# Weight halves through the PSUM bank, third halves in other steps, loads in mid-step: a fused attention and two-MLP kernel

## The chip, the cores and the metric

One core of a Trainium2 chip runs the whole program. The metric is device time in microseconds from the first to the last instruction and what lies around it, as the median of several runs. TensorE (PE) does the matmuls and transposes, VectorE (DVE) and ScalarE (ACT) read and write both memories, GpSimd (POOL) works on SBUF alone, SyncE (SP) issues nearly all DMAs.

## What is computed

Decayed linear attention in blocks, then two MLPs in a row, all in float32 (the kernel splits each float32 matmul operand in a high and a low part and adds three products):

```python
x = _attn_ref(q, k, v, lam)          # B=2, H=8, S=768, D=64; state decays by lam per position
x = x.transpose(0, 2, 1, 3).reshape(1536, 512)
h = x @ w_in;  g = h * clip(h + 3, 0, 6) / 6;  x = g @ w_out          # 1536x512 -> 2048 -> 512
h = x @ w2_in; P = a0 + a1*h + a2*h**2 + a3*h**3
Q = 1 + |b0|*|h| + |b1|*h**2; out = (P / (Q + 1e-6)) @ w2_out
```

The weights arrive as 64-bit floats. The kernel loads the two 32-bit words of each and builds a float32 from them on ScalarE and VectorE.

## The kernel before

Attention runs over 12 chunks of 128 tokens (CH = 128, NCH = 12, six chunks for each batch entry). The first MLP runs in blocks of 512 tokens (TB), so the first block can start when four chunks (CPT) are done. The work has three stretches. A prologue does chunks 0 to 4 and the first projections. Then a loop `for s in range(1, att_steps)` (s = 1 to 7) overlaps one attention chunk c = 4 + s with one projection mm1(s + 1), one output product mm2(s - 1) and the weight conversion for later steps. Behind it a stage of mm1 and mm2 alone runs through the rest of both MLPs. The document counts steps by s.

Everything stands under `tc.manual_schedule()`: each engine runs its instructions in the order in which the code issues them, and waits are set from the tiles that they read and write. So the order of calls in a step is the order in each engine's queue.

**TensorE in a step**: mm1(s + 1) (12 matmuls, L232, into the bank hb[(s + 1) % 2]), att_t (eight transposes of q and k into the banks X and Y, L368 and L373), the first half of mm2(s - 1) (L248), att_s (scores into X and Y, L405), att_q (query times carried state, L425, into both hb banks; not for chunk 6), att_kv (key times value, L434, into the upper half of hb[(s + 1) % 2]; not for chunks 5 and 11), att_v (masked scores times v, L443, into both hb banks), the second half of mm2. In the loop `ba` is hb[(s + 1) % 2] and `bb` is hb[s % 2].

**The others**: act1 is relu on ScalarE (L281) and a product on VectorE (L284); att_t runs between them and has two ScalarE copies, qT (L369) and kT (L374). att_m is two products with the decay mask on VectorE (L412). att_qd (L391) multiplies qT by the decay table on GpSimd; its result qd is read by att_q. att_kd (L381) does the same for k. att_x copies the chunk's output out of the two hb banks (ScalarE L466, VectorE L468). att_state updates the carried state from the bank (VectorE L452 or L454) and decays it on GpSimd (L457). act_fin splits the activation in high (ScalarE L293) and low (GpSimd L294).

**Weight jobs**: job j (j of 2 or more) holds one slice of w_in, part (j, 0), for mm1(j), and one of w_out, part (j, 1), for mm2(j - 2). load_job puts both DMAs on SyncE's queue, into the raw buffers raw0 and raw1, two of each. A part goes through four calls:

- conv_c: the upper words, scaled by ScalarE (L167), clamped by VectorE (L169), into the tile ta (w_in) or tb (w_out), two buffers each.
- the low bits: conv_l has ScalarE write them into a PSUM bank (L179) and VectorE shift and merge from there (L182); the raw buffer is then free. conv_s has ScalarE write them over the raw words (L194) and VectorE merge from SBUF (L196); the sign is read from the raw buffer later.
- conv_w: VectorE merges the sign (L206).
- conv_h: ScalarE casts to the high part (L219), GpSimd subtracts for the low part (L220).

A step takes two parts, pa and pb, from a list, and in the steps named in MORE a third one, pc, at its end. `held` keeps parts whose conv_h comes in the next step. Jobs are loaded at the end of a step, one job ahead of the next part that is due.

In the page's names the tiles of the splits and halves appear as wih and wil (high and low of w_in), woh and wol, gh and gl.

Of the kernel before, what the change touches and what calls it, by code (L numbers as in the profile page):

```python
# [10 lines left out]
U32 = mybir.dt.uint32  # L11
BF16 = mybir.dt.bfloat16
AF = mybir.ActivationFunctionType
ALU = mybir.AluOpType
# [5 lines left out]
LAG2 = 3  # L20
WARM = (8, 3, 2, 4)
EARLY_LOW = 3
MORE = (5, 6)
SIGN = 0x80000000


# [6 lines left out]
def fused_kernel(  # L33
# [14 lines left out]
    nc = tc.nc  # L48
# [4 lines left out]
    KD = DM // 128  # L53
# [99 lines left out]
    def conv_c(j, i, late=False, part=None):  # L153

        if i >= len(jobs[j]):
            return
        if part == "clamp":
            x = conv[j, i]
            nc.vector.tensor_scalar(out=x, in0=x, scalar1=CMAX, scalar2=-CMAX, op0=ALU.min, op1=ALU.max)
            return  # L160
        m = jobs[j][i][0]
        if late:
            x = rp.tile([128, KD, 128, 2], U32, name="raw0").bitcast(F32)
            x = x.rearrange("p k f t -> p (k f t)")[:, 0 : KD * 128].rearrange("p (k f) -> p k f", k=KD)
        else:
            x = tp.tile([128, KD, 128], F32, name="ta" if m % 2 == 0 else "tb")
        nc.scalar.activation(x, raw[j][i].bitcast(F32)[:, :, :, 1], AF.Copy, scale=EXPO)  # L167
        if part is None:
            nc.vector.tensor_scalar(out=x, in0=x, scalar1=CMAX, scalar2=-CMAX, op0=ALU.min, op1=ALU.max)  # L169
        conv[j, i] = x  # L170

    def conv_l(j, i, bank=None, part=None):
# [11 lines left out]
        )  # L184
        conv[j, i] = x, y, x.bitcast(U32)

    def conv_s(j, i, half=None):

        if i >= len(jobs[j]):
            return  # L190
        x = conv[j, i][0] if half else conv[j, i]
        y, r = x.bitcast(U32), raw[j][i]
        if not half:
            nc.scalar.activation(r[:, :, :, 0], r[:, :, :, 0], AF.Copy, scale=LOWS, bias=LOWB)  # L194
        k = slice(0, KD) if half is None else slice(KD // 2 * half, KD // 2 * half + KD // 2)
        nc.vector.scalar_tensor_tensor(  # L196
            out=y[:, k], in0=y[:, k], scalar=3, in1=r[:, k, :, 0], op0=ALU.logical_shift_left, op1=ALU.bitwise_or
        )
        conv[j, i] = x, y, r[:, :, :, 1]

    def conv_w(j, i):

        if i >= len(jobs[j]):
            return
        x, y, sg = conv[j, i]
        nc.vector.scalar_tensor_tensor(  # L206
            out=x.bitcast(U32), in0=sg, scalar=SIGN, in1=y, op0=ALU.bitwise_and, op1=ALU.bitwise_or
        )

    def conv_h(j, i):  # L210

        if i >= len(jobs[j]):
            return
        m, f = jobs[j][i]
        hi, lo = W["out" if m % 2 else "in", f]
        x = conv.pop((j, i))[0]
        if m % 2:
            x = x.rearrange("p a b -> p (a b)")
        nc.scalar.copy(hi, x)  # L219
        nc.gpsimd.tensor_tensor(lo, x, hi.bitcast(F32), op=ALU.subtract)  # L220
# [68 lines left out]
    def act_fin(s):  # L289
        if s in fin:  # L290
            g = fin.pop(s)
            gh, gl = g_tiles(s)
            nc.scalar.copy(gh, g)  # L293
            nc.gpsimd.tensor_tensor(gl, g, gh.bitcast(F32), op=ALU.subtract)  # L294
# [27 lines left out]
    with ExitStack() as actx:  # L322
# [15 lines left out]
        def load_nat(c, which):  # L338
            b, s0 = c // CPB, (c % CPB) * CH
            for nm in which:  # L340
                if c < CPT:
                    x = pp.tile([128, H, D], F32, name=f"{nm}n{c}")
                else:
                    x = ap.tile([128, H, D], F32, name=nm + "n", bufs=2)
                src = {"q": q, "k": k, "v": v}[nm]
                src = src[b, :, s0 : s0 + CH, :]
                if nm == "v":
                    nc.sync.dma_start(x, src.rearrange("h s d -> s h d"))
                else:

                    for e in range(2):
                        nc.sync.dma_start(x[:, 4 * e : 4 * e + 4], src[e::2].rearrange("h s d -> s h d"))
                nat.setdefault(c, {})[nm] = x
# [23 lines left out]
        def att_kd(c):  # L377
            kd = None
            if c % CPB != CPB - 1:
                kd = ap.tile([128, H, D], F32, name="kd", bufs=2)  # L380
                nc.gpsimd.tensor_tensor(  # L381
                    kd, nat[c]["k"], ktab.unsqueeze(2).to_broadcast([128, H, D]), op=ALU.mult
                )
            kds[c] = kd
# [63 lines left out]
        def att_state(c):  # L448
            if c % CPB == CPB - 1:
                return  # L450
            if c % CPB:
                nc.vector.tensor_tensor(state, decayed["S"], kvs[c], op=ALU.add)  # L452
            else:
                nc.vector.tensor_copy(state, kvs[c])  # L454
            if c % CPB != CPB - 2:
                sd = ap.tile([128, NP, D], F32, name="sd")
                nc.gpsimd.tensor_tensor(sd, state, qtab[:, :, CH - 1 : CH].to_broadcast([128, NP, D]), op=ALU.mult)  # L457
                decayed["S"] = sd

        def att_x(c, out):  # L460
            del live[c]
            o = CH * (c % CPT)
            hi, lo = (x[c // CPT][:, :, o : o + CH].rearrange("p (g h) i -> p h g i", h=2) for x in (xh, xl))
            xs = [x[:, 0 : 2 * CH].rearrange("p (g i) -> p g i", g=2) for x in out]
            for h in range(2):
                nc.scalar.copy(hi[:, h], xs[h])  # L466
            for h in range(2):
                nc.vector.tensor_tensor(lo[:, h], xs[h], hi[:, h].bitcast(F32), op=ALU.subtract)  # L468

        with tc.manual_schedule():  # L470
# [99 lines left out]
                conv_w(2, 0)  # L570

            act1(0, between)
            att_x(CPT, (X, Y))
            att_state(CPT)
            conv_c(2, 1)
            conv_h(2, 0)
            conv_l(2, 1, acc[2])
            conv_w(2, 1)
            act_fin(0)
            load_nat(6, "v")  # L580
            load_job(4)
            mm1(1)
# [4 lines left out]

            att_steps = NCH - CPT
            parts = [(j, i) for j in range(3, att_steps + 3) for i in range(2)]
            loaded, held = 4, []  # L590
            for s in range(1, att_steps):
                c = CPT + s
                ba, bb = hb[(s + 1) % 2], hb[s % 2]
                n = 3 if s in MORE else 2
                (pa, pb, *pc), parts = parts[:n], parts[n:]
                conv_c(*pa)
                if s == 1:
                    conv_l(*pa, acc[3], "low")
                    conv_h(2, 1)
                    conv_l(*pa, acc[3], "shift")  # L600
                else:
                    conv_l(*pa, bb)
                    conv_w(*pa)
                    for p in held:
                        conv_h(*p)
                    held = []
                    conv_c(*pb)
                    conv_s(*pb)
                att_kd(c)
                mm1(s + 1)  # L610
                act1(s + 1, lambda: att_t(c, (X, Y)))
                if s == 1:
                    conv_w(*pa)
                    conv_c(*pb)
                else:
                    conv_w(*pb)
                att_qd(c)
                if c + 2 < NCH:
                    load_nat(c + 2, "qk")
                mm2(s - 1, (0, 1))  # L620
                conv_h(*pa)
                if s == 1:
                    act_fin(1)
                else:
                    conv_h(*pb)
                act_fin(s + 1)
                att_s(c, (X, Y))
                for h in range(2):
                    att_m(c, (X, Y), h)
                att_q(c, (bb, ba), True)  # L630
                att_kv(c, ba[:, D * NP :])
                att_v(c, (bb, ba), False)
                if c + 2 < NCH:
                    load_nat(c + 2, "v")
                mm2(s - 1, (2, 3))
                att_x(c, (bb, ba))
                att_state(c)
                if s == 1:
                    conv_s(*pb)
                    conv_w(*pb)  # L640
                    held = [pb]
                for p in pc:
                    conv_c(*p)
                    conv_l(*p, ba)
                    conv_w(*p)
                    held.append(p)
                done = parts[0][0] if parts else att_steps + 3
                while loaded < min(done + 1, att_steps + 3):
                    loaded += 1
                    load_job(loaded)  # L650
            nc.sync.dma_start(a_sb, a_dram.unsqueeze(0).to_broadcast([128, 4]))
            nc.sync.dma_start(b_sb, b_dram.unsqueeze(0).to_broadcast([128, 2]))
            nc.scalar.activation(b1a, b_sb[:, 1:2], AF.Abs)
# [105 lines left out]
```

## Time and profile before

| | us |
|---|---|
| median of 3 runs | 593.75 (593.49 to 594.12) |
| the profiled execution | 591.63 |
| its span | 589.9 |
| TensorE matmuls busy | 578.7 |
| VectorE, ScalarE, GpSimd busy | 433.1, 386.4, 362.2 |

The granted TensorE clock is 1.00 over the whole span. TensorE is busy nearly all the time as an average, but its ends are modelled, so a busy row does not say by itself that no time is lost: the pitch from one step's first matmul to the next step's does. In a timeline row the first number is the start in us, the second the length, then engine, line, operation, output and inputs, and the count of merged instructions; in square brackets stands the idle time of that engine just before it and what ended it.

### The profile page before, as it was taken

What the parts mean: (1) busy time and instruction counts of PE and PEld (TensorE: products, weight loads), DVE (VectorE), ACT (ScalarE), POOL (GpSimd) and SP (SyncE); (2) the same over time, 40 slices, a digit from 0 to 9 for tenths busy, and PEclk for the clock granted to TensorE, in tenths of its full rate; (3) what the DMA queues carried; (4) which work ended last, traced back from release to release, by engine and by line L of the source; (5) the groups of instructions that cost most, each with busy time, mean ns of one, the idle gap of its engine ahead of it and who ended that gap; (6) DMA issues with size and microseconds to landing.
All of it is one profiled execution on the core that took longest, in us unless ns stands there. A gap on an engine that the chain in (4) does not pass through costs nothing.

```text
span 589.9 us, 8862 instructions
## 1 busy us (share of the span) xinstructions
PE 578.7 (98%) x3313; PEld 474.1 (80%) x3313; DVE 433.1 (73%) x478; ACT 386.4 (66%) x650; POOL 362.2 (61%) x290
## 2 busy tenths in 40 slices
PE   8999998999999999999999999999999999999996
PEld 6777786788888888888888888888888888888885
DVE  6688778587310111688888999999998988899990
ACT  3586667676422222678787888888876677877761
POOL 2775866566312222367666778788767767777771
PEclk9999999999999999999999999999999999999999
DMA  9997675353000000465664001000100000100001
GB/s 187 255 256 215 164 220 174 109 174 111 0 1 0 1 0 1 142 201 167 205 177 145 1 1 36 1 1 1 72 1 0 1 1 2 72 0 1 1 1 72
DMA packets 61676, 46.73 MB, mean 79 GB/s; under 512 B 39488, under 2 KB 56128, under 8 KB 61632
## 3 DMA queue, kind: packets, MB, share of 16 engines
q1 hardware_dynamic: 61344, 46.02, 27.7%
q8 instruction: 26, 0.43, 0.3%
q14 instruction: 18, 0.15, 0.1%
q10 hardware_dynamic: 288, 0.14, 0.1%
HBM read 43.00 MB, written 3.15 MB: 78 GB/s over the span
## 4 chain that ended last, share of the span: by engine, by line
PE 87%; DVE 1%; ACT 1%; DMA 1%; issue 1%; DVEq 0%; ACTq 0%
PE acc L248 43%; PE hb L232 42%; PE hb L443 1%; DMA raw<-in_moe_w_in_dram 1%; PE X L405 1%; PE hb L434 0%; DVE tb L206 0%; PE hb L425 0%; DVE at L412 0%; PE X L368 0%; PE Y L373 0%; DVE td L284 0%; ACT tc L281 0%; ACT raw L194 0%; DVE tb L196 0%
## 5 line engine op out<-in xcount | busy, mean ns | idle before, releaser
L317 DVE RECIPROCAL Y<-tb 128x512 f32<-128x512 f32 x48 | 161.3, 3361 | 1.6
L294 POOL TENSOR_TENSOR gl<-td,gh 128x512 fp32r<-128x512 f32 x84 | 108.7, 1295 | 82.8 <-ACT gh L293 82.8
L232 PE MATMUL hb<-xh,wih 128*128 128x512 f32 x384 | 102.9, 390 | 0.2 <-ACT wih L219 0.2
L232 PE MATMUL hb<-xl,wih 128*128 128x512 f32 x384 | 102.7, 389 | 0.0
L232 PE MATMUL hb<-xh,wil 128*128 128x512 f32 x384 | 102.6, 389 | 0.0
L308 POOL TENSOR_TENSOR tc<-ta,tc 128x512 f32<-128x512 f32 x48 | 62.2, 1297 | 55.4 <-ACT tc L305 55.4
L284 DVE SCALAR_TENSOR_TENSOR td<-tc,hb 128x512 f32<-128x512 f32 x48 | 32.8, 684 | 85.0 <-ACT tc L281 85.0
L232 PEld LDWEIGHTS hb<-xh,wih 128*128 128x128 f32 x384 | 71.9, 188 | 15.5 <-ACT wih L219 0.5
L232 PEld LDWEIGHTS hb<-xl,wih 128*128 128x128 f32 x384 | 72.1, 188 | 15.0
L232 PEld LDWEIGHTS hb<-xh,wil 128*128 128x128 f32 x384 | 72.1, 188 | 15.0
L281 ACT ACTIVATE tc<-hb,c 128x512 f32<-128x512 f32 x48 | 32.9, 685 | 69.3 <-PE hb L232 69.1
L248 PE MATMUL acc<-gh,woh 128*128 128x512 f32 x192 | 76.1, 396 | 0.0
L248 PE MATMUL acc<-gh,wol 128*128 128x512 f32 x192 | 74.9, 390 | 0.5 <-POOL wol L220 0.5
L248 PE MATMUL acc<-gl,woh 128*128 128x512 f32 x192 | 74.8, 390 | 0.0
L293 ACT CAST gh<-td 128x512 fp32r<-128x512 f32 x84 | 51.7, 616 | 25.1 <-DVE td L284 13.5
L309 POOL TENSOR_TENSOR td<-td,tc 128x512 f32<-128x512 f32 x48 | 64.3, 1339 | 3.8
L220 POOL TENSOR_TENSOR wil<-ta,wih 128x512 fp32r<-128x512 f32 x32 | 43.1, 1348 | 26.8 <-ACT wih L219 25.9
L302 ACT ACTIVATE X<-hb,b_sb 128x512 f32<-128x512 f32 x48 | 31.8, 662 | 39.3 <-PE hb L232 36.6
L248 PE MATMUL acc<-woh,gh 128*128 128x512 f32 x144 | 56.0, 389 | 0.0
L248 PE MATMUL acc<-wol,gh 128*128 128x512 f32 x144 | 56.0, 389 | 0.0
L248 PE MATMUL acc<-woh,gl 128*128 128x512 f32 x144 | 56.0, 389 | 0.0
L220 POOL TENSOR_TENSOR wol<-tb,woh 128x512 fp32r<-128x512 f32 x29 | 38.0, 1309 | 22.8 <-ACT woh L219 22.8
(141 smaller groups left out, 1005.8 us busy)
## 6 DMA issues: line engine op xcount, KB each, us to landing
raw<-in_moe_w_in_dram SPq DMA_DIRECT2D x32, 512.0 KB, 4.0
raw<-in_moe_w_out_dram SPq DMA_DIRECT2D x32, 512.0 KB, 4.6
qn<-in_q_dram SPq DMA_DIRECT2D x24, 128.0 KB, 3.7
kn<-in_k_dram SPq DMA_DIRECT2D x24, 128.0 KB, 3.8
vn<-in_v_dram SPq DMA_DIRECT2D x12, 256.0 KB, 4.4
out_dram<-raw SPq DMA_DIRECT2D x11, 256.0 KB, 2.0
out_dram<-raw ACTq DMA_DIRECT2D x1, 128.0 KB, 1.8
out_dram<-raw SPq DMA_DIRECT2D x1, 128.0 KB, 2.5
```

Source lines behind the costliest of these rows:

```text
L220: nc.gpsimd.tensor_tensor(lo, x, hi.bitcast(F32), op=ALU.subtract)
L232: nc.tensor.matmul(h, lhsT=w[:, kk, :], rhs=x[:, kk, :], start=i == 0 and kk == 0, stop=i == 2 and kk == KD - 1)
L248: nc.tensor.matmul(acc[d], lhsT=l, rhs=r, start=st and i == 0, stop=sp and i == 2)
L281: nc.scalar.activation(t, h, AF.Relu, bias=c3)
L284: nc.vector.scalar_tensor_tensor(out=g, in0=t, scalar=6.0, in1=h, op0=ALU.min, op1=ALU.mult)
L293: nc.scalar.copy(gh, g)
L294: nc.gpsimd.tensor_tensor(gl, g, gh.bitcast(F32), op=ALU.subtract)
L302: nc.scalar.activation(X, h, AF.Abs, scale=b_sb[:, 0:1])
L308: nc.gpsimd.tensor_tensor(b1, h2, b1, op=ALU.mult)
L309: nc.gpsimd.tensor_tensor(a1, a1, b1, op=ALU.add)
L317: nc.vector.reciprocal(Y, q1)
L405: nc.tensor.matmul(bk[h2][t, 128 * p : 128 * p + 128], lhsT=kT[r, p, t], rhs=qT[r, p, :], start=True, stop=True)
```

## The change

Second parts pb no longer use conv_s ahead of the relu. A new function conv_m has ScalarE write their low bits into the bank bb behind att_t, and VectorE merge from there; the sign (conv_w, now called by `done`) follows behind att_x, and conv_h in the next step. MORE is (4, 6) instead of (5, 6), and third parts use conv_s at the end of their step. conv_h of held parts is split: the first goes ahead of conv_c(pb), the rest between the two calls of conv_m. att_kd for a chunk moves to the end of the step before. load is called after act1 and at the end of a step; `left` holds the parts whose sign merge is not yet issued, and jobs are loaded up to one past the first of them. In step 1 conv_c(pb) moves ahead of mm1, and act_fin(1) ahead of att_qd. In the prologue att_x and att_state of chunk 4 move behind the conversion of part (2, 1). Behind the loop the remaining held parts get their conv_h.

```diff
-MORE = (5, 6)
+MORE = (4, 6)
+    def conv_m(j, i, bank, part):
+        if i >= len(jobs[j]):
+            return
+        x, r = conv[j, i], raw[j][i]
+        low = bank.bitcast(U32).rearrange("p (a b) -> p a b", a=KD)
+        if part == "low":
+            nc.scalar.activation(low, r[:, :, :, 0], AF.Copy, scale=LOWS, bias=LOWB)
+            return
+        y = x.bitcast(U32)
+        nc.vector.scalar_tensor_tensor(
+            out=y, in0=y, scalar=3, in1=low, op0=ALU.logical_shift_left, op1=ALU.bitwise_or
+        )
+        conv[j, i] = x, y, r[:, :, :, 1]
@@ prologue
             act1(0, between)
-            att_x(CPT, (X, Y))
-            att_state(CPT)
             conv_c(2, 1)
             conv_h(2, 0)
             conv_l(2, 1, acc[2])
             conv_w(2, 1)
+            att_x(CPT, (X, Y))
             act_fin(0)
+            att_state(CPT)
@@ ahead of the loop
-            loaded, held = 4, []
+            held = []
+            att_kd(CPT + 1)
+            left, loaded = list(parts), [4]
+            def load():
+                while loaded[-1] < min((left[0][0] if left else att_steps + 3) + 1, att_steps + 3):
+                    loaded.append(loaded[-1] + 1)
+                    load_job(loaded[-1])
+            def done(p):
+                conv_w(*p)
+                left.remove(p)
@@ the loop
                 else:
                     conv_l(*pa, bb)
-                    conv_w(*pa)
-                    for p in held:
-                        conv_h(*p)
-                    held = []
-                    conv_c(*pb)
-                    conv_s(*pb)
-                att_kd(c)
+                    done(pa)
+                for p in held[:1]:
+                    conv_h(*p)
+                conv_c(*pb)
                 mm1(s + 1)
                 act1(s + 1, lambda: att_t(c, (X, Y)))
                 if s == 1:
-                    conv_w(*pa)
-                    conv_c(*pb)
-                else:
-                    conv_w(*pb)
+                    done(pa)
+                    act_fin(1)
+                load()
+                conv_m(*pb, bb, "low")
+                for p in held[1:]:
+                    conv_h(*p)
+                conv_m(*pb, bb, "shift")
                 att_qd(c)
...
                 conv_h(*pa)
-                if s == 1:
-                    act_fin(1)
-                else:
-                    conv_h(*pb)
                 act_fin(s + 1)
...
                 att_x(c, (bb, ba))
+                done(pb)
+                held = [pb, *pc]
+                if c + 1 < NCH:
+                    att_kd(c + 1)
                 att_state(c)
-                if s == 1:
-                    conv_s(*pb)
-                    conv_w(*pb)
-                    held = [pb]
+                if not pc:
+                    load()
                 for p in pc:
                     conv_c(*p)
-                    conv_l(*p, ba)
-                    conv_w(*p)
-                    held.append(p)
-                done = parts[0][0] if parts else att_steps + 3
-                while loaded < min(done + 1, att_steps + 3):
-                    loaded += 1
-                    load_job(loaded)
+                    conv_s(*p)
+                    done(p)
+                    load()
+            for p in held:
+                conv_h(*p)
```

## Rows read from the trace of the kernel before

**Rows 1.** TensorE's timeline: first projection matmuls of steps 2 to 7 and behind.
```profile
44.44 1.07 PE L232 MATMUL hb<-xh,wih 128*128 128x512 f32 x4
...
54.82 1.07 PE L232 MATMUL hb<-xh,wih 128*128 128x512 f32 x4
...
64.53 1.07 PE L232 MATMUL hb<-xh,wih 128*128 128x512 f32 x4
...
74.25 1.07 PE L232 MATMUL hb<-xh,wih 128*128 128x512 f32 x4
...
83.97 1.07 PE L232 MATMUL hb<-xh,wih 128*128 128x512 f32 x4
...
95.72 1.07 PE L232 MATMUL hb<-xh,wih 128*128 128x512 f32 x4
...
106.54 1.07 PE L232 MATMUL hb<-xh,wih 128*128 128x512 f32 x4
```

**Rows 2.** TensorE's timeline: waits in steps 1, 2, 6, 7; L425 of step 4.
```profile
41.76 1.25 PE L443 MATMUL hb<-at,vn 128*64 128x128 f32 x16 [0.34 <-DVE at L412]
...
52.14 1.26 PE L443 MATMUL hb<-at,vn 128*64 128x128 f32 x16 [0.92 <-DVE at L412]
...
70.54 0.62 PE L425 MATMUL hb<-qd,state 64*64 64x128 f32 x16
...
91.02 0.33 PE L405 MATMUL X<-qT,kT 64*64 64x128 f32 x2 [1.90 <-ACT kT L374]
...
101.78 0.33 PE L405 MATMUL X<-qT,kT 64*64 64x128 f32 x2 [0.91 <-ACT kT L374]
...
103.86 1.26 PE L443 MATMUL hb<-at,vn 128*64 128x128 f32 x16 [0.48 <-DVE at L412]
```

**Rows 3.** ScalarE's timeline in step 4.
```profile
64.35 0.64 ACT L179 ACTIVATE hb<-raw 128x512 uint32<-128x512 uint32 x1 [0.24 <-DVE state L452]
...
67.52 0.69 ACT L281 ACTIVATE tc<-hb,c 128x512 f32<-128x512 f32 x1 [1.37 <-PE hb L232]
...
69.05 0.64 ACT L219 CAST wih<-ta 128x512 fp32r<-128x512 f32 x1
```

**Rows 4.** VectorE's timeline in step 4.
```profile
65.76 0.69 DVE L206 SCALAR_TENSOR_TENSOR ta<-ta,hb 128x512 uint32<-128x512 uint32 x1
66.36 0.42 DVE L169 TENSOR_SCALAR tb<-tb 128x512 f32<-128x512 f32 x1
...
68.84 1.75 DVE L206 SCALAR_TENSOR_TENSOR tb<-raw,tb 128x512 uint32<-128x512 uint32 x1
70.83 0.69 DVE L412 TENSOR_TENSOR at<-X,dmat 128x512 f32<-128x512 f32 x1 [0.23 <-PE Y L405]
```

**Rows 5.** GpSimd's timeline: qd of step 1, then step 4.
```profile
38.41 1.29 POOL L391 TENSOR_TENSOR qd<-qT,qtab 128x512 f32<-128x512 f32 x1
...
68.76 1.28 POOL L391 TENSOR_TENSOR qd<-qT,qtab 128x512 f32<-128x512 f32 x1 [2.48 <-ACT qT L369]
70.00 1.74 POOL L220 TENSOR_TENSOR wil<-ta,wih 128x512 fp32r<-128x512 f32 x1
...
72.92 1.30 POOL L294 TENSOR_TENSOR gl<-td,gh 128x512 fp32r<-128x512 f32 x1
```

**Rows 6.** ScalarE's timeline: copy of kT in step 1, then step 6.
```profile
38.12 0.60 ACT L374 COPY kT<-Y 128x512 f32<-128x512 f32 x1
...
88.21 0.67 ACT L167 ACTIVATE ta<-raw 128x512 f32<-128x512 f32 x1 [1.12 <-DMA raw<-in_moe_w_in_dram]
...
89.33 0.68 ACT L281 ACTIVATE tc<-hb,c 128x512 f32<-128x512 f32 x1
```

**Rows 7.** SyncE's timeline: the first load of job 8, end of step 4.
```profile
73.33 0.53 SPq L142 DMA_DIRECT2D raw<-in_moe_w_in_dram  x1
```

**Rows 8.** DMA issues between 73.3 and 73.8 us: count, KB, us to landing.
```profile
raw<-in_moe_w_in_dram SPq DMA_DIRECT2D x1, 512.0 KB, 4.7
```

**Rows 9.** Busy by engine, granted clock, DMA share, GB/s, behind the last matmul.
```profile
588.00:589.00 1.00, 0.00 (x0) 0.00 (x0) 0.00 (x0) 0.00 (x0) 0.00 (x0) 1.00 0.02 7
```

More of the change, by code (lines that the diff above doesn't have):

```diff
@@ L191, in conv_s @@
         x = conv[j, i][0] if half else conv[j, i]
-        y, r = x.bitcast(U32), raw[j][i]
+        r = raw[j][i]
         if not half:
             nc.scalar.activation(r[:, :, :, 0], r[:, :, :, 0], AF.Copy, scale=LOWS, bias=LOWB)
+        y = x.bitcast(U32)
         k = slice(0, KD) if half is None else slice(KD // 2 * half, KD // 2 * half + KD // 2)
```

## The prediction

> **What bounds the kernel now.** I read the timeline of TensorE first, for the first projection matmul of each step of the overlapped loop and of the stage behind it [rows 1]. Behind 106.54 us the chain of waits holds only TensorE matmuls, back to back, up to the output stores, and the change issues nothing there except one late weight split; so I count only the loop. Its steps 3, 4 and 5 start at 54.82, 64.53, 74.25 and end at 83.97: 9.7 us each, with no idle on TensorE. That is the floor of a full step. Step 2 took 10.38, step 6 11.75, step 7 10.82 us. Step 2 has no inter-chunk product (L425) and step 7 no key-value product (L434), so their floors are lower still.
>
> Second, the same timeline's waits [rows 2]: step 1 waits for VectorE's mask product at 41.76, step 2 at 52.14, step 6 for ScalarE's copy of kT at 91.02 (1.90 us), step 7 at 101.78. So TensorE bounds the kernel, and what can be won is the stalls of steps 1, 2, 6 and 7: nearly 4 us above 9.7 in the last three, and more against their lower floors. Third, the queues of the other engines in step 4, where everything fits [rows 3 to 5], then in the steps that stall [rows 6]. I count u, time since the step's first projection matmul; step 4 starts at 64.53.
>
> **The floor of a step, for placing the new work.** ScalarE's relu starts at u = 2.99, the operation behind the copies of qT and kT at 4.52 [rows 3]. TensorE's L425, first writer of the banks hb and reader of qd, starts at 6.01, and 3.71 us later the next step begins [rows 1, 2]. The first mask product starts at 6.30 [rows 4]. GpSimd's qd product runs from 4.23 to 5.51, right behind the copy of qT [rows 5]. So qd has 0.5 us to spare; whatever goes ahead of it on GpSimd shows on TensorE.
>
> **Second halves through the bank (conv_m).** Removed: the in-place ScalarE pass of conv_s ahead of the relu, and VectorE's sign merge L206 between the relu product and the mask products. That merge took 1.75 us in step 4 against 0.69 us for the one at 65.76, which reads a bank [rows 4]; it ended 0.55 us behind GpSimd's qd, which ran from 68.76 to 70.04, and the GpSimd operation behind it took 1.74 instead of 1.3 [rows 5]: operands that are all in SBUF make the two engines wait for each other, those with a bank don't. Added: a ScalarE pass into hb behind the copy of kT (u = 4.52 to 5.16, 0.64 us by the pass at 64.35 [rows 3]) and a shift on VectorE (0.69, 5.2 to 5.9). New wait: L425 writes this bank, so it waits for that shift. 5.9 against 6.01 is a tie: 0 to 0.05 us in each of steps 3, 4 and 6. I take 0.05 for all three together.
>
> The merge itself moves behind the output copies (att_x), ahead of the state update. There it meets GpSimd's split or kd product and ends 0.6 us after it at worst, near u = 0.4 of the next step. Queued behind it: the state update, and behind that ScalarE's low pass of the next first half, which wants the same bank. ScalarE then has three operations of 0.56 each (89.33 less 88.21, halved [rows 6]) before the relu, ending at about 2.4; relu at 2.99: hidden, with 0.5 us left. The second half's hi cast and lo subtraction move into the next step; they end near 3.3, and mm2 wants the low part at about 3.8. Hidden.
>
> Step 2 gains: the wait at 52.14 (u = 7.70; step 2 starts at 44.44 [rows 1, 2]) came from the mask product queued behind the slow merge. Without it that product ends at 6.30 + 0.69, so L443 starts at 7.04: −0.63 us (bounds −0.4 and −0.8).
>
> **Step 1: act_fin(1) moves ahead of att_qd.** This puts the split of g (ScalarE cast, then GpSimd L294) in front of qd on GpSimd's queue. ScalarE also gets conv_c of the second half ahead of the relu, 0.5 us more before kT: its copy starts at 38.6 instead of 38.12 [rows 6]. Cast 39.1 to 39.7, split 1.30 to 41.0, qd 1.28 to 42.3, where it started at 38.41 before [rows 5]. L425 then starts at 42.3, and L443 some 0.55 later (an estimate: L425's busy 0.62 less the overlap of its end), 42.87 instead of 41.76 [rows 2]: +1.1 us (0.9 to 1.2).
>
> **MORE = (4, 6) and the loads.** The third half now comes at the end of steps 4 and 6, by conv_s, with no wait for the bank. Step 6 needs weight job 9; its load goes out in mid-step 5, as soon as the raw buffers are free, not at the end of it. That removes the stall of step 6, whose ScalarE copy at 88.21 had waited for this transfer [rows 6]: step 6 falls from 11.75 to 9.78, −1.97 us.
>
> But step 5 now needs the first half of job 8 as its second part, and job 8 is still loaded at the end of step 4: left[0] is (7, 1) only after the third half is done. On SyncE the load stands behind the load of v, goes out at 73.33 as before [rows 7] and lands 4.7 us later [rows 8], at u = 3.8 of step 5. conv_c of that part stands ahead of the relu on ScalarE, so the relu goes from 2.99 to 4.4 and the copy of kT ends at 6.0.
>
> **Third halves' splits ahead of qd.** held[1:], set in steps 4 and 6, is split in steps 5 and 7 between the two parts of conv_m. Its GpSimd subtraction is issued ahead of att_qd and waits for a ScalarE cast that itself stands behind kT's copy and the low pass. GpSimd runs in order, so qd, which could start behind qT's copy, waits for all of that.
> Step 5: kT's copy issued at 5.44, low pass 5.92, cast 6.49 to 7.1, subtraction to 8.4, qd to 9.7; L425 at 9.73 instead of 6.01: +3.7 us. If the load landed early, the pass would still wait for the bank, freed at about 5.5 by the first half's merge: +3.3. Bounds 3.3 and 3.75.
> Step 7: relu on time. The low pass starts at 4.52 if the bank is free, at 5.15 if VectorE is late: behind the second half's merge it has the state update, two clamps (0.42), two shifts and two merges (0.69 to 0.73) [rows 4], 4.0 us in all, and one GpSimd subtraction of 1.3 that may get in between, 0.05 + 4.0 to 5.3. L425 follows at 8.35 to 8.95. Then 0.55 and, from L443 on, 2.68 (106.54 less 103.86 [rows 1, 2]): 11.58 to 12.18 instead of 10.82, +0.76 to +1.36. Middle: +1.06.
>
> The other moves cost nothing: att_kd of the next chunk goes to the end of a step, into GpSimd time that the second half's subtraction has left (cover gone: at most its own 1.3 us before the state product); att_x and att_state of the prologue run later, with the banks X and Y free about 0.9 us before the transposes that write them. The q and k loads that now stand behind mid-step weight loads on SyncE are needed a step later. The last split behind the loop has several us until mm2 reads it.
>
> **Sum**: +1.11 − 0.63 + 0.05 + 3.72 − 1.97 + 1.06 = +3.3 us on the profiled execution's 591.63 (span 589.9), which lies 2.1 us under the median of the runs. On the median of 593.75: **597.0 us**. With the bounds: +2.2 to +4.1, 595.9 to 597.8.
>
> **Rivals.**
> Faster: qd is not late. It decides at the start of qd: if GpSimd is free by u = 4.7 in steps 5 and 7 (and by 39.5 us in step 1), the queue costs nothing. Then step 1 is unchanged, step 5 loses 1.35 to the load and the bank, step 7 falls to about 9.9: −0.63 + 1.35 − 1.97 − 0.9 = −2.15, 591.6 us. For it: GpSimd is idle for over 2 us ahead of qd in an ordinary step. Against: the operation ahead is fed by ScalarE after kT's copy, and the trace has GpSimd strictly in program order. 0.13.
> Near no change: the waits in steps 5 and 7 are right, but half of them is swallowed by something that I placed too late: 0 to +1.2 us, 594.4. 0.09.
> The tie lost: ScalarE 0.3 us late in each of the three ordinary steps, L425 waits for the bank each time: +0.9 more, 597.9. 0.07.
> The change doesn't do what it says: job 9's raw buffer is freed so late (its sign is now read from it at the end) that the load is no earlier; step 6 keeps its 1.97: 599.0. Step 5 itself is then 13.4 us long, which speaks against it. 0.04.
> The clock: the granted clock is still 1.00 between 588 and 589 us, well behind the last matmul [rows 9]; the new gaps are 2.6 us or less. The Trainium skill, "TensorE: Matmul & The Clock Gate", Part 1, says that an idle TensorE is put back to half rate. By that rule the gaps of steps 5 and 7 would let the clock fall from 2.4 to 1.2 GHz. What it would do here by the rows: the 3.7 us from L425 to the end of the step would take twice as long, twice, +7.4 us, 604. 0.02.
>
> **How the numbers follow.** Forecast 0.65, rivals 0.13, 0.09, 0.07, 0.04, 0.02. A measurement of this kernel can tell about 0.2%, 1.2 us, from no change. Slower: 0.65 + 0.07 + 0.04 + 0.02 and nothing of the near case, 0.78; within: 0.09; faster 0.13. The range leaves out the faster rival and the lower half of the near one below, and the clock above: 594.4 to 599.0.
>
> **What would show it.** Right: step 5 about 13.4 us long, its L425 waiting for GpSimd's qd, qd directly behind an L220 subtraction; step 7 the same at 12; step 6 back at 9.7 with no DMA wait on ScalarE; L206 of second halves behind L468; qd of step 1 behind L294. Wrong: qd ahead of these subtractions, or L425 in step 5 before u = 8, or ordinary steps over 9.8.

## The result, and the profile after

The changed kernel took 597.41 us (median of 4 runs, 596.97 to 598.28) against 593.62 for the kernel before beside it (593.23 to 594.12): a ratio of 1.0065, 95% interval 1.0048 to 1.0083. Slower, by 3.8 us. Its profiled execution took 597.40, with a span of 595.7 us. One of the 12 runs of fill_gap, below, took 837.41 us at a mean granted clock of 0.655 and is left aside; no trace of it is kept, and its cause is open.

Its lines have moved: mm1 is L248, mm2 L264, att_s L421, att_q L441, att_kv L450, att_v L459; relu L297, copies of qT and kT L385 and L390, low pass of conv_m L194 and its shift L197, sign merge L222, casts and subtractions of conv_h L235 and L236, split of g L309 and L310, qd L407. In the other kernels the numbers differ by a few lines; the tiles tell which operation it is.

TensorE's timeline, first projection matmuls of steps 2 to 7 and behind, as in [rows 1]:

```profile
45.68 1.07 PE L248 MATMUL hb<-xh,wih 128*128 128x512 f32 x4
...
55.33 1.07 PE L248 MATMUL hb<-xh,wih 128*128 128x512 f32 x4
...
64.97 1.09 PE L248 MATMUL hb<-xh,wih 128*128 128x512 f32 x4
...
74.62 1.07 PE L248 MATMUL hb<-xh,wih 128*128 128x512 f32 x4
...
89.67 1.07 PE L248 MATMUL hb<-xh,wih 128*128 128x512 f32 x4
...
99.30 1.07 PE L248 MATMUL hb<-xh,wih 128*128 128x512 f32 x4
...
113.02 1.10 PE L248 MATMUL hb<-xh,wih 128*128 128x512 f32 x4
```

The differences between them are the step lengths. All kernels of this study, in us from the first projection matmul of a step to that of the next, each from its profiled execution (u is the time since that first matmul, as in the prediction). The ratio is to the runs of the kernel before that were made beside each: 593.62 us for the changed kernel, 593.04 for qd_first to before_fill, 592.83 for before_fin1 to thirds_late.

| kernel | 1 | 2 | 3 | 4 | 5 | 6 | 7 | median of runs, us | ratio to before |
|---|---|---|---|---|---|---|---|---|---|
| before | 10.39 | 10.38 | 9.71 | 9.72 | 9.72 | 11.75 | 10.82 | 593.62 | 1 |
| after | 11.36 | 9.65 | 9.64 | 9.65 | 15.05 | 9.63 | 13.72 | 597.41 | 1.0065 |
| qd_first | 10.28 | 9.65 | 9.65 | 9.65 | 10.85 | 9.65 | 10.34 | 589.07 | 0.9937 |
| load8_early | 11.36 | 9.64 | 9.65 | 9.65 | 14.49 | 9.62 | 13.72 | 596.66 | 1.0059 |
| fill_gap | 11.35 | 9.65 | 9.65 | 9.64 | 13.23 | 9.65 | 12.16 | 594.00 | 1.0017 |
| before_fill | 10.31 | 10.39 | 9.71 | 9.71 | 9.72 | 12.98 | 10.80 | 592.42 | 0.9991 |
| before_fin1 | 11.44 | 10.40 | 9.70 | 9.70 | 9.70 | 11.99 | 10.82 | 594.34 | 1.0025 |
| late9 | 10.31 | 9.62 | 9.63 | 9.65 | 11.12 | 12.01 | 10.34 | 591.57 | 0.9983 |
| qd_first_load8 | 10.28 | 9.65 | 9.64 | 9.65 | 10.81 | 9.67 | 10.32 | 588.65 | 0.9933 |
| thirds_late | 10.29 | 9.64 | 9.63 | 9.64 | 9.74 | 9.64 | 9.63 | 586.94 | 0.9904 |

The change won 0.73 us in step 2, 0.07 in each of steps 3 and 4 and 2.12 in step 6, and paid 0.97 in step 1, 5.33 in step 5 and 2.90 in step 7. TensorE's timeline, the waits that answer to [rows 2]:

```profile
42.57 0.67 PE L441 MATMUL hb<-qd,state 64*64 64x128 f32 x16 [1.42 <-POOL qd L407]
...
52.65 1.26 PE L459 MATMUL hb<-at,vn 128*64 128x128 f32 x16 [0.16 <-DVE at L428]
...
80.86 0.33 PE L421 MATMUL X<-qT,kT 64*64 64x128 f32 x2 [1.08 <-ACT kT L390]
...
84.51 0.67 PE L441 MATMUL hb<-qd,state 64*64 64x128 f32 x16 [2.55 <-POOL qd L407]
...
108.34 0.67 PE L441 MATMUL hb<-qd,state 64*64 64x128 f32 x16 [2.85 <-POOL qd L407]
```

In steps 1, 5 and 7 L441 waits for GpSimd's qd; in the kernel before it waited for it nowhere in the loop. GpSimd's timeline in the same three steps says why:

```profile
40.01 1.28 POOL L310 TENSOR_TENSOR gl<-td,gh 128x512 fp32r<-128x512 f32 x1 [1.38 <-ACT gh L309]
41.25 1.26 POOL L407 TENSOR_TENSOR qd<-qT,qtab 128x512 f32<-128x512 f32 x1
...
81.96 1.27 POOL L236 TENSOR_TENSOR wil<-ta,wih 128x512 fp32r<-128x512 f32 x1 [4.22 <-ACT wih L235]
83.19 1.26 POOL L407 TENSOR_TENSOR qd<-qT,qtab 128x512 f32<-128x512 f32 x1
...
105.79 1.27 POOL L236 TENSOR_TENSOR wol<-tb,woh 128x512 fp32r<-128x512 f32 x1 [3.12 <-ACT woh L235]
107.02 1.27 POOL L407 TENSOR_TENSOR qd<-qT,qtab 128x512 f32<-128x512 f32 x1
```

Each time GpSimd sat idle (1.38, 4.22, 3.12 us) in front of a subtraction that waited for a ScalarE cast, and qd stood behind it. ScalarE's timeline in step 5, then the low pass of step 7:

```profile
78.60 0.67 ACT L167 ACTIVATE ta<-raw 128x512 f32<-128x512 f32 x1 [2.22 <-DMA raw<-in_moe_w_in_dram]
79.17 0.68 ACT L297 ACTIVATE tc<-hb,c 128x512 f32<-128x512 f32 x1
...
80.69 0.67 ACT L194 ACTIVATE hb<-raw 128x512 uint32<-128x512 uint32 x1
81.26 0.63 ACT L235 CAST wih<-ta 128x512 fp32r<-128x512 f32 x1
...
104.51 0.66 ACT L194 ACTIVATE hb<-raw 128x512 uint32<-128x512 uint32 x1 [0.63 <-DVE ta L222]
```

Read downwards, the first four lines are the chain of step 5: the load of job 8 lands and is converted from u = 3.98, then relu, the copies (not shown), low pass, cast; the cast releases the subtraction at 81.96.

One thing stands in this profile that the rows of before did not have. Busy time by second of TensorE alone, with the granted clock (length, TensorE busy and count, clock, DMA share, GB/s):

```profile
84.00:85.00 1.00, 0.49 (x16) 1.00 1.30 210
85.00:86.00 1.00, 1.00 (x28) 0.73 0.27 44
86.00:87.00 1.00, 1.00 (x12) 0.50 0.06 16
87.00:88.00 1.00, 1.00 (x9) 0.50 0.00 0
88.00:89.00 1.00, 1.00 (x4) 0.57 0.07 17
89.00:90.00 1.00, 1.00 (x6) 1.00 1.02 233
```

Behind the gap of step 5 the clock fell from 2.4 GHz to half, 1.2 GHz, until shortly before 89 us. It did not fall in the gap: L441 had started at 84.51, and the clock was still whole until about 85.5. Behind the gap of step 7, where L441 started at 108.34, it did so again, until shortly before 113 us:

```profile
107.00:108.00 1.00, 0.00 (x0) 1.00 0.01 0
108.00:109.00 1.00, 0.66 (x18) 1.00 0.00 0
109.00:110.00 1.00, 1.00 (x16) 0.67 0.00 0
110.00:111.00 1.00, 1.00 (x7) 0.50 0.00 0
...
112.00:113.00 1.00, 1.00 (x4) 0.62 0.00 0
```

### The profile page after: what moved, and what is told of

Same layout as the page of the kernel before. It is cut to its first block, busy times and chain, and to the rows that moved or that the text cites. A ratio compares the mean times of both kernels' runs of the same rounds, so it can differ in the third digit from the quotient of the medians.

```text
span 595.7 us, 8871 instructions
## 1 busy us (share of the span) xinstructions
PE 581.6 (98%) x3313; PEld 476.8 (80%) x3313; DVE 429.9 (72%) x478; ACT 384.9 (65%) x650; POOL 359.7 (60%) x290
## 3 DMA queue, kind: packets, MB, share of 16 engines
HBM read 43.00 MB, written 3.15 MB: 77 GB/s over the span
## 4 chain that ended last, share of the span: by engine, by line
PE 83%; issue 2%; POOL 1%; DVE 1%; ACT 1%; POOLq 0%; ACTq 0%
PE acc L264 42%; PE hb L248 40%; PE hb L459 1%; POOL qd L407 0%; PE hb L441 0%; DVE ta L222 0%; PE hb L450 0%; POOL wil L236 0%; DVE ta L212 0%; PE X L421 0%; ACT tb L167 0%; ACT hb L179 0%; ACT raw L209 0%; ACT wih L235 0%; PE X L384 0%
## 5 line engine op out<-in xcount | busy, mean ns | idle before, releaser
L310 POOL TENSOR_TENSOR gl<-td,gh 128x512 fp32r<-128x512 f32 x84 | 108.5, 1292 | 83.7 <-ACT gh L309 83.7
L248 PE MATMUL hb<-xh,wih 128*128 128x512 f32 x384 | 102.9, 390 | 0.2 <-ACT wih L235 0.2
L248 PE MATMUL hb<-xl,wih 128*128 128x512 f32 x384 | 102.7, 389 | 0.0
L248 PE MATMUL hb<-xh,wil 128*128 128x512 f32 x384 | 102.6, 389 | 0.0
L248 PEld LDWEIGHTS hb<-xh,wih 128*128 128x128 f32 x384 | 72.0, 188 | 15.6 <-ACT wih L235 0.5
L248 PEld LDWEIGHTS hb<-xl,wih 128*128 128x128 f32 x384 | 72.1, 188 | 15.0
L248 PEld LDWEIGHTS hb<-xh,wil 128*128 128x128 f32 x384 | 72.1, 188 | 15.0
L297 ACT ACTIVATE tc<-hb,c 128x512 f32<-128x512 f32 x48 | 32.8, 683 | 68.5 <-PE hb L248 68.5
L264 PE MATMUL acc<-gh,woh 128*128 128x512 f32 x192 | 77.0, 401 | 0.0
L264 PE MATMUL acc<-gh,wol 128*128 128x512 f32 x192 | 75.6, 394 | 0.4 <-POOL wol L236 0.4
L264 PE MATMUL acc<-gl,woh 128*128 128x512 f32 x192 | 75.2, 392 | 0.0
L309 ACT CAST gh<-td 128x512 fp32r<-128x512 f32 x84 | 52.0, 619 | 25.1 <-DVE td L300 13.5
L236 POOL TENSOR_TENSOR wil<-ta,wih 128x512 fp32r<-128x512 f32 x32 | 41.6, 1301 | 35.4 <-ACT wih L235 35.4
L264 PE MATMUL acc<-woh,gh 128*128 128x512 f32 x144 | 56.0, 389 | 0.0
L264 PE MATMUL acc<-woh,gl 128*128 128x512 f32 x144 | 56.0, 389 | 0.0
L264 PE MATMUL acc<-wol,gh 128*128 128x512 f32 x144 | 56.0, 389 | 0.0
L236 POOL TENSOR_TENSOR wol<-tb,woh 128x512 fp32r<-128x512 f32 x29 | 37.5, 1293 | 23.7 <-ACT woh L235 22.7
```

The lines of the kernel that those rows point to most:

```text
L248: nc.tensor.matmul(h, lhsT=w[:, kk, :], rhs=x[:, kk, :], start=i == 0 and kk == 0, stop=i == 2 and kk == KD - 1)
L264: nc.tensor.matmul(acc[d], lhsT=l, rhs=r, start=st and i == 0, stop=sp and i == 2)
L297: nc.scalar.activation(t, h, AF.Relu, bias=c3)
```

## The experiments

Theory: GpSimd ran its operations in the order of issue, and work put ahead of qd that waits for ScalarE delays L441. Rivals: the late load of job 8, the wait for conv_m's bank, and the clock as a cause of its own.

**qd_first**: the changed kernel, only the order of qd undone.

```diff
                 act1(s + 1, lambda: att_t(c, (X, Y)))
+                att_qd(c)
                 if s == 1:
                     done(pa)
                     act_fin(1)
...
                 conv_m(*pb, bb, "shift")
-                att_qd(c)
```

> The changed kernel with att_qd issued directly behind act1, so ahead of the held part's split in steps 5 and 7 and ahead of act_fin(1) in step 1; nothing else differs. Queue theory (qd stood behind other GpSimd work): step 1 falls from 11.36 to about 10.4 us, step 5 from 15.05 to about 11.2 (what is left is the late load of job 8 and the bank), step 7 from 13.72 to about 10.0, no gap over 1.5 us, granted clock 1.00: 8.5 us less than the changed kernel, about 589 us. Load theory (step 5 is long because job 8 lands late): step 5 stays over 13, about 594. Bank theory (L425 waits for conv_m's shift): steps 5 and 7 stay as they are.

Measured: 589.07 us, ratio 0.9937 (0.9923 to 0.9951), clock 0.999 or 1.00 in all runs; steps 1, 5 and 7 at 10.28, 10.85 and 10.34. TensorE's waits in steps 5 and 7:

```profile
79.36 0.33 PE L421 MATMUL X<-qT,kT 64*64 64x128 f32 x2 [0.74 <-ACT kT L390]
...
80.73 0.67 PE L441 MATMUL hb<-qd,state 64*64 64x128 f32 x16 [0.27 <-DVE ta L197]
...
101.11 0.67 PE L441 MATMUL hb<-qd,state 64*64 64x128 f32 x16 [0.98 <-DVE tb L197]
```

One line moved takes 8.3 us off the median and turns a loss of 0.65% into a gain of 0.63%. Some 3 of the 8.3 are the two falls of the clock (fill_gap, below), which go with the gaps; the rest is the shorter wait. The load theory wanted step 5 over 13, the bank theory no change: both fall as the main cause. Both are still seen as small waits: 0.74 us for kT, held up by the load, and 0.27 and 0.98 for the bank.

**load8_early**: the changed kernel, first load of job 8 in mid-step 4.

```diff
                 load()
+                if s == MORE[0]:
+                    loaded[-1] += 1
+                    load_job(loaded[-1], (0,))
                 conv_m(*pb, bb, "low")
...
+                if s == MORE[0]:
+                    load_job(loaded[-1], (1,))
                 if not pc:
                     load()
```

> The changed kernel with the first load of job 8 issued in mid-step 4 instead of at its end; order of GpSimd as in the changed kernel. Queue theory: ScalarE's relu in step 5 comes back to u = 3, but the low pass waits for the bank until u = 5.5, so qd comes only 0.5 us earlier: step 5 14.5 instead of 15.05, about 597 us. Load theory: step 5 falls to about 10, and its clock fall is gone, about 592 us.

Measured: 596.66 us, ratio 1.0059 (1.0045 to 1.0073), step 5 at 14.49. TensorE's timeline in step 5:

```profile
83.80 0.73 PE L443 MATMUL hb<-qd,state 64*64 64x128 f32 x16 [3.21 <-POOL qd L409]
```

The wait for kT is gone and the wait for qd has grown by 0.66 instead: ScalarE's relu is on time (u = 2.92), but its low pass waits for the bank until u = 5.56. Early loading alone takes 0.56 us off step 5: the load is not the main cause.

**fill_gap**: the changed kernel with filler matmuls in the two gaps; their results are not used.

```diff
                 att_s(c, (X, Y))
+                if s in (5, 7):
+                    warm_up(10 if s == 5 else 10, ba)
```

> The changed kernel with ten matmuls on the warm-up tile, into a bank that is free there, behind att_s in steps 5 and 7, in the gaps of 2.55 and 2.85 us in which TensorE waited for qd. They compute nothing that is used. If the clock fell because of these gaps: granted clock 1.00, step 5 13.6 instead of 15.05, step 7 12.3 instead of 13.72, 594.5 us. If the two falls have another cause or cost nothing: 597.4 us as before.

Measured: 594.00 us, ratio 1.0017 (1.0008 to 1.0025), clock 0.999 or 1.00; steps 5 and 7 at 13.23 and 12.16. TensorE's timeline, L441 of step 5 and the next step:

```profile
84.16 0.67 PE L441 MATMUL hb<-qd,state 64*64 64x128 f32 x16 [0.30 <-POOL qd L407]
...
87.74 1.09 PE L248 MATMUL hb<-xh,wih 128*128 128x512 f32 x4
```

qd came nearly as late (L441 at u = 9.65 and 9.05, where it had been 9.89 and 9.04), but the clock stayed. So the two gaps made the clock fall. By the medians the falls cost 3.4 us between them (597.41 less 594.00), which includes 0.24 for the earlier qd of step 5 and the scatter between the two sets of runs. The rows say 3.15: from L441 of step 5 to the next step it took 5.16 us in the changed kernel (84.51 to 89.67) and 3.58 in this one, and in step 7 4.68 and 3.11.

**before_fill**: the kernel before with fillers in the gap of step 6.

```diff
                 act_fin(s + 1)
+                if s == 6:
+                    warm_up(8, bb)
                 att_s(c, (X, Y))
```

> The kernel before with eight matmuls on the warm-up tile ahead of att_s in step 6, in the gap of 1.90 us in which TensorE waited for kT. If most runs of the kernel before lose clock behind that gap (its profiled execution with a clock of 1.00 took 591.63 us, the median 593.62): about 592 us at a clock of 1.00. If the difference between them is something else: 593.6 us, no change.

Measured: 592.42 us, ratio 0.9991 (0.9982 to 1.0001), mean clock 0.998 to 1.00 in its 12 runs. The runs of the kernel before beside it fall in two groups: 13 of 23 had a mean clock of 0.996 or 0.997 and took 593.0 to 594.0 us, 10 had 0.998 to 1.00 and took 591.6 to 592.6. With the fillers the first group is gone, so those runs lost their clock behind the gap of step 6. No profile was taken of such a run: that the fall itself lies there is concluded from the fillers. In time the edit is not clearly a gain over all runs of the kernel before; its median lies in the range of their second group. Its profiled execution was the slowest of the 12, at 593.1 us: there the load of job 9 was waited for until u = 5.46, where it had been 4.24 in [rows 6], so step 6 took 12.98. ScalarE's timeline there:

```profile
89.77 0.68 ACT L167 ACTIVATE ta<-raw 128x512 f32<-128x512 f32 x1 [2.34 <-DMA raw<-in_moe_w_in_dram]
```

**before_fin1**: the kernel before with one part of the change, act_fin(1) ahead of att_qd.

```diff
                 if s == 1:
                     conv_w(*pa)
                     conv_c(*pb)
+                    act_fin(1)
                 else:
                     conv_w(*pb)
                 att_qd(c)
...
-                if s == 1:
-                    act_fin(1)
-                else:
+                if s > 1:
                     conv_h(*pb)
```

> The kernel before with only one part of the change: in step 1 act_fin(1) ahead of att_qd. Queue theory: qd starts about 2.2 us later, at 40.6 instead of 38.41, L425 at 41.9, step 1 grows from 10.39 by some 0.5 to 1.0 us, the other steps keep their lengths (10.38, 9.71, 9.72, 9.72, 11.75, 10.82); the time is 0.5 to 1 us over the kernel before. If the split ahead of qd doesn't matter: step 1 stays 10.4.

Measured: 594.34 us, ratio 1.0025 (1.0015 to 1.0036); step 1 at 11.44, 1.05 more than before; steps 2 to 5 and 7 as before. GpSimd's, then TensorE's timeline in step 1:

```profile
40.38 1.27 POOL L294 TENSOR_TENSOR gl<-td,gh 128x512 fp32r<-128x512 f32 x1 [1.42 <-ACT gh L293]
41.61 1.26 POOL L391 TENSOR_TENSOR qd<-qT,qtab 128x512 f32<-128x512 f32 x1
```
```profile
42.93 0.67 PE L425 MATMUL hb<-qd,state 64*64 64x128 f32 x16 [1.45 <-POOL qd L391]
```

The same pair of rows as in step 1 of the changed kernel, from this edit alone. The median is 1.5 us over that of the kernel before beside it (592.83), more than step 1 explains and than was expected; what the rest is stays open.

**late9**: qd_first without the mid-step load of step 5.

```diff
-                load()
+                if s != 5:
+                    load()
                 conv_m(*pb, bb, "low")
```

> qd_first with the mid-step load of step 5 taken out, so job 9 is loaded at the end of step 5 as in the kernel before. If the mid-step load is what cured step 6: ScalarE waits for the load again, step 6 grows from 9.65 to 10.8 to 11.6, about 590.6 us. If step 6 was cured by the smaller work ahead of its relu: step 6 stays 9.65 and the time 589.07.

Measured: 591.57 us, ratio 0.9983 (0.9971 to 0.9996), step 6 at 12.01. TensorE's timeline in step 6:

```profile
91.48 0.33 PE L421 MATMUL X<-qT,kT 64*64 64x128 f32 x2 [1.91 <-ACT kT L390]
```

The wait of [rows 2] at 91.02 is back, at its old size, and with it the kernel takes 2.5 us more than qd_first in the median. So the mid-step load is what cured step 6, not the lighter ScalarE queue; leaving it out cost 0.4 us more in step 6 than I had written.

**qd_first_load8**: both edits shown above, together.

> Both edits together: att_qd directly behind act1, and the first load of job 8 in mid-step 4. In qd_first step 5 still took 10.85 us against 9.65 for an ordinary step; TensorE waited 0.74 for kT (ScalarE had waited for the load) and 0.27 for conv_m's shift. Load theory: the load is what is left, step 5 falls to 9.7, 1.1 us less than qd_first, 588.0 us. Bank theory: VectorE frees the bank only at u = 5.5, because the third half's merge stands ahead of the first half's; then the load hides behind that, L425 comes 0.3 earlier, 588.8 us, hardly to be told from 589.07.

Measured: 588.65 us, ratio 0.9933 (0.9921 to 0.9946); step 5 at 10.81. ScalarE's timeline in step 5:

```profile
79.09 0.66 ACT L196 ACTIVATE hb<-raw 128x512 uint32<-128x512 uint32 x1 [1.00 <-DVE tb L224]
```

The relu is on time, and ScalarE waits for the bank instead, as the bank theory had it.

**thirds_late**: as qd_first_load8, with the VectorE part of the third half behind the first half's.

```diff
                 conv_c(*pb)
+                for p in held[1:]:
+                    conv_s(*p, part="shift")
+                    done(p)
                 mm1(s + 1)
...
                 for p in pc:
                     conv_c(*p)
-                    conv_s(*p)
-                    done(p)
-                    load()
+                    conv_s(*p, part="low")
```

> As qd_first_load8, and the third half's shift and merge on VectorE moved from the end of steps 4 and 6 to behind the first and second part's work in steps 5 and 7, so that the bank is free at about u = 3. If VectorE's order and the load are all that is left in steps 5 and 7: 9.7 instead of 10.85 and 9.2 instead of 10.34, 2.2 us less than qd_first, 586.9 us. If the added work ahead of the relu product pushes the shift or the mask products out: no gain, 589 or more.

Measured: 586.94 us, ratio 0.9904 (0.9891 to 0.9918), steps 5 and 7 at 9.74 and 9.63; step 7 did not come down to the 9.2 expected. TensorE's timeline between 70 and 110 us has one wait left in the loop:

```profile
99.64 1.26 PE L463 MATMUL hb<-at,vn 128*64 128x128 f32 x16 [0.19 <-DVE at L432]
```

That is 10.5 us less than the changed kernel and 5.9 us less than the kernel before beside it (592.83), with every idea of the change kept.

## Why the prediction was right, and where it was not

**The sign and the mechanism were right.** Forecast 597.0 us, measured 597.41; the steps that it named are the steps that grew and shrank, and qd_first shows that the queue in front of qd decided it. That the point came out within half a microsecond is luck, as shown below.

By its own terms, step for step (L441 or the step length, forecast against measured):

- Step 1: +1.11 against +0.97, and +1.05 with that edit alone.
- Step 2: −0.63 against −0.73. The slow merge, of the kind that takes 1.75 us in [rows 4], went from between the relu product and the mask products; TensorE's wait fell from 0.92 to 0.16.
- Ordinary steps: 0 to +0.05 in all for the tie between conv_m's shift and L441; measured −0.07 in each of steps 3 and 4. VectorE's timeline in step 4:

```profile
70.19 0.69 DVE L197 SCALAR_TENSOR_TENSOR tb<-tb,hb 128x512 uint32<-128x512 uint32 x1 [0.80 <-ACT hb L194]
71.20 0.69 DVE L428 TENSOR_TENSOR at<-X,dmat 128x512 f32<-128x512 f32 x1 [0.32 <-PE Y L421]
...
73.99 0.83 DVE L222 SCALAR_TENSOR_TENSOR tb<-raw,tb 128x512 uint32<-128x512 uint32 x1
```

  The shift ends at u = 5.91, L441 starts at 6.05: the tie held. The merge at its new place took 0.83.
- Step 6: −1.97 against −2.12, by the load, as late9 shows.
- Step 5: L441 at u = 9.73 against 9.89.
- Step 7: L441 at u = 8.35 to 8.95 against 9.04, just past the upper end. The GpSimd subtraction that "may get in between" did. VectorE's and GpSimd's timelines:

```profile
100.83 0.69 DVE L222 SCALAR_TENSOR_TENSOR tb<-raw,tb 128x512 uint32<-128x512 uint32 x1
101.44 1.51 DVE L169 TENSOR_SCALAR ta<-ta 128x512 f32<-128x512 f32 x1
```
```profile
101.11 1.56 POOL L236 TENSOR_TENSOR wil<-ta,wih 128x512 fp32r<-128x512 f32 x1 [3.22 <-ACT wih L235]
```

  A clamp that takes 0.42 us elsewhere took 1.51 and ended 0.28 us behind the subtraction, which ran until 102.67. The Trainium skill, "SBUF — State Buffer", Who interferes with whom, says that of these two engines the one that issues first keeps the port pair that they share for its whole instruction, and the other is blocked. The rows agree, and they add that VectorE's operations in a row don't keep GpSimd out: the subtraction became ready during the merge at 100.83 and got in ahead of the clamp.

The prediction held the floors of steps 2 and 7 to be lower than 9.7, with no figure and no term of the sum on it. They are hardly lower: with waits of 0.16 and 0.19 us left, these steps took 9.64 and 9.63 us in thirds_late, as long as the full ones there.

**The clock was judged wrongly, and the point forecast is right partly because two errors cancel.** The rival got 0.02, with the argument that the clock was still 1.00 behind the last matmul [rows 9]. That row could not show it: it looks at an idle TensorE with no matmul behind it, and in the changed kernel the clock was still 1.00 in the gaps too and fell only when TensorE had been at work again for about a microsecond. Step 5 has two gaps, 1.08 and 2.55 us, with one microsecond of work between; step 7 has a single one of 2.85. What the prediction cited there from the Trainium skill ("TensorE: Matmul & The Clock Gate", Part 1), that an idle TensorE is put back to half rate, is what these rows show, behind gaps of 2.55 and 2.85 us. Its price was mis-sized as well: 1.6 us in step 5 (5.16 against 3.58 from L441 to the next step) and 1.5 in step 7 (113.02 less 108.34, against 104.30 less 101.11 in qd_first), not 3.7 each, since the clock came back before the stretch was over.

On the profiled executions the sum was +3.3 and the span grew by 5.8, from 589.9 to 595.7. Without the 3.1 of the two falls the loop grew by 3.1, close to the sum; the rest is 0.3 us in the prologue and a tail that ended 0.7 sooner behind the last matmul. On the medians it is 3.8, because the kernel before's profiled execution (591.63 us, clock 1.00) lies 2.0 us under its median. About 1.3 of them are what its runs at a clock of 0.996 or 0.997 lose against the others beside before_fill (593.5 against 592.2 on average); the four runs beside the result, 593.23 to 594.12, lie with the slower group by their times; their clocks are not on record. The rest is scatter. The prediction carried a sum made on a profile without a fall over to a median with one, and left out two falls on the other side. Carried on from the profiled execution alone, the sum would have given 594.9, and 597.40 was measured.

What stays open: what decides which executions of the kernel before lose their clock. With the fillers of before_fill, which left 1.39 us of the gap in step 6 idle, no run did; but the profiled execution of the kernel before and that of late9 have gaps of 1.90 and 1.91 us there and no fall.

## What to carry to other kernels

On an engine that runs in order, an operation that something waits for should be issued ahead of any that only has to be done some time, even if the latter looks ready: here one line, moved up, was worth 8.3 us, the clock included. When work is moved, write down for each queue what then stands behind it, and who waits for that; the change had gains of 2.1 and 0.7 us that were real and hidden under one such order. And a gap on TensorE can cost more than its length: here those of 2.55 and 2.85 us were each followed by a fall of the clock that cost another 1.5 to 1.6 us.

## What the runs showed of the hardware

- In the profile of the changed kernel the granted clock fell to half behind gaps of 2.55 and 2.85 us, about a microsecond after TensorE had started again, and cost 1.5 to 1.6 us each time. It may not do so in every execution: one of the six runs of load8_early had a mean clock of 0.997 instead of 0.993 or 0.994 and took 1.4 us less than the others, as if one of its two falls were missing. Behind the gap of about 1.9 us in step 6 of the kernel before it fell in some executions and not in others, by their mean clocks.
- Matmuls that compute nothing, put into the gaps, kept the clock and took 3.4 us off the median.
- The same 512 KB weight load behind the same v load was waited for until u = 4.24 in the profile of the kernel before and 5.46 in that of before_fill, which differ only in matmuls issued behind it: a load that lands on the path can move a step by more than a microsecond (11.75 against 12.98 us).
